# A gated mix of an S4 convolution and a GEGLU network: the feed-forward's gate and up products moved beside the making of K, and folded input spectra

## The chip, the cores and the metric

The kernel runs on one core of a Trainium2 chip. The metric is the device time of one execution in microseconds (us). A span is the same execution as the profile sees it; it is some 2 us shorter. Each run is labelled fast or slow. Only fast runs enter the ratios.

The engines are called as in the profile: PE multiplies matrices (PEld loads its weights), DVE works on vectors, ACT evaluates functions and copies, POOL here issues the indirect transfers, SP issues most DMA transfers (SPq is its queue).

## The reference

```python
x = A_u                                            # 1 x 2048 x 640, bf16
g = sigmoid((x * gate_w).sum(-1, keepdims=True))
K = einsum("dn,dnl,dn->dl", C, exp(dt*A*l), dt*B).real      # 640 channels, 128 complex modes each
y = irfft(rfft(x padded to 4096) * rfft(K padded to 4096))[:2048]   # per channel
a = y + x * Dskip
b = (gelu(x @ w_gate) * (x @ w_up)) @ w_down       # 640 -> 1728 -> 640
return g * a + (1 - g) * b
```

Both kernels make K from tables of exponentials and sines (ACT), scale them (DVE), and contract over the 128 modes with very small matmuls (PE), 160 channels at a time. The convolution is done with four blocks of 512 tokens: spectra of x (called U) and of K by matmuls with a table of cosines and sines, products of spectra on DVE, and an inverse transform by matmuls again.

## The kernel before

K is made first, with the transform of x beside it. The contraction of 160 channels is 320 matmuls, each of 21 columns with a weight load of its own. Its result is copied and laid out anew by 16 small transfers.

```python
    def contract(ch):                                   # called four times
        ...
        for hb in range(2):
            for g in range(gh):
                for q in range(2):
                    for j in range(4):
                        d = G4 * j + gh * hb + g
                        nc.tensor.matmul(psK[32 * j:32 * j + 32, hb, NX2 * g:NX2 * g + NX2], lhsT=cs1[:, q, :, d],
                                         rhs=cs2[:, q, :, d], start=(q == 0), stop=(q == 1))

    def k_out(ch):
        ...                                             # two ACT copies out of PSUM
        for j in range(4):
            for q in range(4):
                na = 6 if q == 0 else 5
                eng = nc.gpsimd if ch == NCH - 1 and j >= 2 else nc.sync
                eng.dma_start(out=Kt[32 * q:32 * q + 32, 0:na, CH * ch + G4 * j:CH * ch + G4 * j + G4],
                                  in_=kst[32 * j:32 * j + 32, q:NX2:4, :])
```

The transform of x takes 256 matmuls with four row blocks each (`for k in range(4)`). When K is there, DVE forms the products of the spectra while PE does gate and up for one block of 512 tokens after the other:

```python
    for tq in range(NB):
        ...
        for ft in range(NFT):
            ...
            gate(tq, ft, Gs[:])                         # five matmuls, then gelu on ACT
            pU = psU.tile([128, 512], FP32, name="pU")
            for kt in range(NKT):
                nc.tensor.matmul(pU[:], lhsT=Wu[:, kt, f0:f0 + 128], rhs=xT[tq][:, kt, :],
                                 start=(kt == 0), stop=(kt == NKT - 1))
            nc.scalar.copy(out=Us[:], in_=pU[:])
            nc.vector.tensor_tensor(out=ht[:, ft, :], in0=Gs[:], in1=Us[:], op=ALU.mult)
```

Last come `down` (28 matmuls per tile of 128 tokens) and the inverse. The inverse uses a symmetry: 128 matmuls give a tile and its mirror image, DVE adds and subtracts the halves, and the mirrored rows are stored by indirect transfers from POOL.

## Time and profile before

The time before is 405.9 us in the median (403.6 to 406.6, four runs). The page of the profiled run begins as follows. The first lines give busy time, share and instructions of each engine. The rows below cut the span into 40 slices, and each digit is a busy share in tenths; PEclk is the granted clock of PE.

```profile
span 404.8 us, 7313 instructions
PE 311.0 (77%) x2903; PEld 181.4 (45%) x2918; DVE 322.1 (80%) x628; ACT 232.8 (58%) x369; POOL 29.0 (7%) x49
...
PE   0556557453565775689999999999999699999993
...
DVE  8979816998765995945999999999994567777753
ACT  7999989858999647347666557465457200100000
...
PEclk9959886665967678679999999999999999999998
```

The windows view gives the same by stage. Its columns are named in its first line.

```profile
core 0: us, PE busy (x) PEld busy (x) DVE busy (x) ACT busy (x) POOL busy (x), PEclk, DMA share, GB/s
...
80.00:120.00 40.00, 22.54 (x579) 16.03 (x572) 33.84 (x79) 33.58 (x66) 0.00 (x0) 0.68 0.17 44
120.00:156.00 36.00, 24.75 (x403) 15.29 (x402) 26.43 (x58) 26.16 (x31) 0.29 (x1) 0.72 0.34 100
...
205.00:313.00 108.00, 103.86 (x541) 49.42 (x551) 103.17 (x151) 64.37 (x108) 3.64 (x4) 1.00 0.07 17
313.00:324.00 11.00, 6.90 (x44) 4.20 (x43) 5.63 (x11) 3.48 (x7) 2.29 (x2) 1.00 0.81 255
324.00:388.00 64.00, 63.99 (x472) 46.10 (x472) 46.20 (x88) 3.84 (x9) 10.36 (x10) 1.00 0.16 52
```

| stage of before, us | what bounds it |
|---|---|
| 0 to 177, K | ACT (busy 142 us) and DVE (138). PE is busy 99 us, at a mean clock of 0.75 |
| 177 to 313, products beside gate and up | both PE (104 of the last 108 us) and DVE (103) |
| 313 to 324 | the load of w_down (DMA share 0.81) |
| 324 to 398, down and inverse | PE, busy 73.8 of 74 us |

### The profile page before, as it was taken

How to read it: one execution, taken by the hardware profiler on the slowest of the kernel's cores; microseconds unless marked ns; L12 is line 12 of the kernel's file. 1: busy time of each engine (PE TensorE's matmuls, PEld its weight loads, DVE VectorE, ACT ScalarE, POOL GpSimd, SP SyncE). 2: the span in 40 equal slices, each digit the busy share in tenths (PEclk: the TensorE clock that was granted, in tenths of full speed). 3: DMA queues.
4: the chain of work that ended last, by engine and by line, in shares of the span. 5: the costliest groups of instructions: out<-in, count | busy, mean ns of one | idle time of the engine just before them, and what ended most of it. 6: DMA issues, size and time to landing. Idle time of an engine off the chain costs nothing.

```text
span 404.8 us, 7313 instructions
## 1 busy us (share of the span) xinstructions
PE 311.0 (77%) x2903; PEld 181.4 (45%) x2918; DVE 322.1 (80%) x628; ACT 232.8 (58%) x369; POOL 29.0 (7%) x49
## 2 busy tenths in 40 slices
PE   0556557453565775689999999999999699999993
PEld 0324222343433454435545445444444377777771
DVE  8979816998765995945999999999994567777753
ACT  7999989858999647347666557465457200100000
POOL 4000000000000001400000000000002204120000
PEclk9959886665967678679999999999999999999998
DMA  6422200021113035372001100100011802121000
GB/s 113 147 78 66 66 6 0 2 70 21 56 27 85 6 105 170 68 215 52 22 0 34 33 1 2 32 2 0 8 34 33 275 27 90 64 68 49 34 34 33
DMA packets 37507, 22.57 MB, mean 56 GB/s; under 512 B 28832, under 2 KB 33632, under 8 KB 37472
## 3 DMA queue, kind: packets, MB, share of 16 engines
q1 hardware_dynamic: 36448, 19.36, 17.6%
q0 software_dynamic: 1024, 2.73, 2.1%
q8 instruction: 23, 0.38, 0.4%
q14 instruction: 12, 0.10, 0.1%
HBM read 14.99 MB, written 2.62 MB: 44 GB/s over the span
## 4 chain that ended last, share of the span: by engine, by line
DVE 33%; PE 32%; ACT 19%; DMA 6%; SPq 5%; issue 4%; POOLq 0%; POOL 0%; ACTq 0%
PE pD L767 13%; PE pG L515 6%; DVE arena L479 5%; DVE arena L478 5%; ACT arena L378 4%; ACT arena L333 4%; PE pU L711 4%; ACT arena L261 3%; DVE arena L715 3%; DVE arena L476 3%; DVE arena L475 3%; PE pY L776 3%; DMA arena<-in_B_w_down_dram 3%; PE psK L410 2%; SPq L424 2%
## 5 line engine op out<-in xcount | busy, mean ns | idle before, releaser
L227 PE MATMUL pT<-arena 128*128 128x320 bf16 x256 | 53.3, 372 | 42.6 <-ACT arena L261 30.0
L515 PE MATMUL pG<-arena 128*128 128x512 bf16 x257 | 65.6, 389 | 4.2 <-DMA arena<-arena 2.2
L711 PE MATMUL pU<-arena 128*128 128x512 bf16 x250 | 65.1, 384 | 1.9 <-DMA arena<-in_B_w_up_dram 1.3
L767 PE MATMUL pD<-arena 128*128 128x320 bf16 x448 | 62.8, 299 | 1.9 <-DMA arena<-in_B_w_down_dram 1.9
L227 PEld LDWEIGHTS <-arena 128*128 128x128 bf16 x256 | 30.2, 119 | 64.6 <-issue 34.9
L767 PEld LDWEIGHTS <-arena 128*128 128x128 bf16 x448 | 43.8, 98 | 19.1 <-issue 2.1
L378 ACT ACTIVATE arena<-arena 128x2240 bf16<-128x2240 int16 (+1 forms) x20 | 43.6, 2180 | 12.0 <-DVE arena L370 7.1
L780 ACT COPY arena<-pY 128x320 f32<-128x320 f32 x16 | 6.8, 426 | 75.7 <-PE pY L776 75.7
L517 ACT ACTIVATE arena<-pG 128x512 bf16<-128x512 f32 x52 | 31.2, 600 | 27.4 <-PE pG L515 26.9
L713 ACT CAST arena<-pU 128x512 bf16<-128x512 f32 x52 | 30.4, 587 | 23.2 <-PE pU L711 21.7
L515 PEld LDWEIGHTS <-arena 128*128 128x128 bf16 x260 | 26.0, 100 | 35.5 <-issue 7.7
L711 PEld LDWEIGHTS <-arena 128*128 128x128 bf16 x260 | 25.3, 98 | 30.5 <-DMA arena<-in_B_w_up_dram 2.2
L410 PE MATMUL psK<-arena 128*32 128x21 bf16 x1280 | 20.7, 213 | 22.9 <-DVE arena L395 8.8
L478 DVE TENSOR_TENSOR arena<-arena 128x1280 bf16<-128x1280 bf16 (+5 forms) x40 | 32.5, 814 | 0.5 <-ACT arena L444 0.5
L479 DVE TENSOR_TENSOR arena<-arena 128x1280 bf16<-128x1280 bf16 (+5 forms) x40 | 32.6, 816 | 0.3
L410 PEld LDWEIGHTS <-arena 128*32 128x32 bf16 x1280 | 20.0, 153 | 24.6 <-issue 15.6
L367 DVE SCALAR_TENSOR_TENSOR arena<-arena 128x160 int32<-128x160 f32 x84 | 20.8, 319 | 11.3 <-ACT arena L378 11.3
L438 PE MATMUL pT<-arena 128*128 128x320 bf16 x144 | 26.7, 318 | 3.3 <-ACT arena L444 2.2
L769 DVE SCALAR_TENSOR_TENSOR arena<-pD,omg,arena 128x320 f32<-128x320 f32 x32 | 17.5, 547 | 14.5 <-PE pD L767 14.5
L444 ACT CAST arena<-pT 128x640 bf16<-128x640 f32 (+1 forms) x40 | 22.6, 592 | 8.0 <-PE pT L438 4.5
L715 DVE TENSOR_TENSOR arena<-arena 128x512 bf16<-128x512 bf16 x52 | 21.5, 414 | 7.0 <-ACT arena L713 7.0
L261 ACT ACTIVATE arena<-pT 128x640 bf16<-128x640 f32 x32 | 21.9, 699 | 5.0 <-PE pT L227 4.3
(97 smaller groups left out, 418.3 us busy)
## 6 DMA issues: line engine op xcount, KB each, us to landing
arena<-in_A_u_dram SPq DMA_DIRECT2D x16, 320.0 KB, 3.3
arena<-in_B_w_gate_dram SPq DMA_DIRECT2D x1, 2160.0 KB, 9.5
arena<-in_B_w_down_dram SPq DMA_DIRECT2D x1, 2080.0 KB, 10.5
arena<-in_B_w_up_dram SPq DMA_DIRECT2D x1, 1360.0 KB, 6.3
arena<-in_A_u_dram SPq DMA_DIRECT2D x8, 160.0 KB, 2.3
out_dram<-arena SPq DMA_DIRECT2D x8, 160.0 KB, 1.8
arena<-in_B_w_up_dram SPq DMA_DIRECT2D x1, 800.0 KB, 5.5
arena<-arena SPq DMA_DIRECT2D x42, 12.5 KB, 1.9
```

The costliest lines, as they stand in the source:

```text
L227: nc.tensor.matmul(pU[:, h, 0:DH], lhsT=tab[:, k, q, fsl(ft)], rhs=ublk[f0, b][:, k, h * DH:(h + 1) * DH], start=(k == 0), stop=(k == 3))
L261: nc.scalar.activation(out=Uf[ft][:, q, b, :].rearrange("p (h d) -> p h d", h=2), in_=pU[:, :, 0:DH], func=ACT.Copy, scale=1.0 / S)
L378: nc.scalar.activation(out=dst, in_=ph_tile(nph[ch, g])[:].bitcast(I16)[:, :, 0:n, 0:2 * CH:2], func=ACT.Sin, scale=SIN_SCALE)
L410: nc.tensor.matmul(psK[32 * j:32 * j + 32, hb, NX2 * g:NX2 * g + NX2], lhsT=cs1[:, q, :, d], rhs=cs2[:, q, :, d], start=(q == 0), stop=(q ...
L478: nc.vector.tensor_tensor(out=t1[:, 0:nb, :], in0=U[:, 1 - q, 0:nb, ds], in1=g[1], op=ALU.mult)
L479: nc.vector.tensor_tensor(out=dst, in0=dst, in1=t1[:, 0:nb, :], op=op1)
L515: nc.tensor.matmul(pG[:], lhsT=Wg[:, kt, 128 * ft:128 * ft + 128], rhs=xT[tq][:, kt, :], start=(kt == 0), stop=(kt == NKT - 1))
L517: nc.scalar.activation(out=out, in_=pG[:], func=ACT.Gelu_apprx_tanh)
L711: nc.tensor.matmul(pU[:], lhsT=Wu[:, kt, f0:f0 + 128], rhs=xT[tq][:, kt, :], start=(kt == 0), stop=(kt == NKT - 1))
L713: nc.scalar.copy(out=Us[:], in_=pU[:])
L715: nc.vector.tensor_tensor(out=ht[:, ft, :], in0=ht[:, ft, :] if early else Gs[:], in1=Us[:], op=ALU.mult)
L767: nc.tensor.matmul(pD[:, 0:DH], lhsT=HT[c][:, ft, 256 * r + par:256 * r + 256:2], rhs=Wd[:, ft, hs], start=(ft == 0), stop=(ft == NFT - 1))
```

## The change

The intent is to fill the half idle PE of the first stage with gate and up, and to pair the products of spectra with the PE work that comes last. All three main engines get a fixed order: a planner places each piece of work by a modelled duration, and a script fixes the sequence of ACT's function tables. The diff is over a thousand lines; this is its core, by hand, with cuts marked.

```diff
+    ctx.enter_context(tc.manual_schedule(engines={ENG.Activation, ENG.DVE, ENG.PE}))
+    plan = Plan()                       # pe(), ve(), ac(), dma(), pool() add pieces with a duration
...
+    def burst(b, banks):                # gate for two of 14 column tiles, all four token blocks, then up
+        for f in (2 * b, 2 * b + 1):
+            for tq in range(NB):
+                gate(f, tq, banks)
...
+        for f in (2 * b, 2 * b + 1):
+            for tq in range(NB):
+                up(f, tq)               # of 8 up results 6 are read from PSUM by DVE, 2 go by an ACT copy
...
+    burst(5, six)
...
+    burst(6, six)
+    for c in range(2, 4):
+        for g in range(3):
+            Z()                         # sine
+            XM2(c, g)                   # scaling
+        contract(c)
...
+    # table of K's transform (FK, 2304 KB) and of cosines (1024 KB): written to DRAM early, read back here
+    dma(430, lambda: nc.sync.dma_start(out=FK..., in_=dFK[:]), r=["dFK"], w=["FK"], after=...)
+    # folded input: natural rows plus and minus mirrored rows
+            pool(1000, lambda ...: nc.gpsimd.indirect_dma_start(out=mir[b][:, h, :], ..., in_=u2[:, :], in_offset=...))
+        ve(..., tensor_tensor(out=pls[b][:], in0=nat[b][:], in1=mir[b][:], op=ALU.add))
+        ve(..., tensor_tensor(out=nat[b][:], in0=nat[b][:], in1=mir[b][:], op=ALU.subtract))
-                for k in range(4):      # transform of x: 256 matmuls
+                        for j in range(2):   # 128 matmuls
...
+    for c in (3, 2, 1, 0):              # products of spectra, block by block, in place of U
+        for ft in range(NF):
+            product(c, ft, hs)
...
-                pE ... e in range(2)    # inverse by symmetric halves, 128 matmuls, mirrored indirect stores
+    for i in range(16): down(i, order[i])
+    for i in range(16): inverse(i, order[i])   # 256 matmuls, 96 small ones for Dskip, plain stores
+    script = [("trig", 8), ("exp", 6), ("gelu", 5), ("sqrt", 1), ("gelu", 3), ("trig", 2), ...]
+    plan.run(script, prio)
+    plan.emit()
```

## The prediction

> **What bounds the kernel now.** The windows view splits the 404.8 us span in three. To about 205 us K is made: ACT is busy 160 us and DVE 160 us, PE only 127 us at a granted clock of 0.59 to 0.83 until 176 us. From 205 to 313 us the chain of waits is nearly all DVE products, DVE busy 50 of 50 us, with PE's gate and up products beside them. From 313 us PE bounds: a 10.5 us wait for w_down, then 28 matmuls of 3.80 us and 8 of 1.09 us alternating to 388 us. After the last indirect store is issued (391.6 us) 13 us pass.
>
> **The change.** Gate and up (about 1.08 us per group of 5 matmuls, 108 groups or 117 us) move into the K stage, whose PE is half idle. The products then run beside w_down and the inverse transform, not beside gate/up.
>
> Stage A, K plus gate/up, at start-to-start rates from the chain (2,560-column sin 2.3, 320-column exp 0.36, 512-column eviction 0.5, bf16 2,560-column multiply 1.40 us):
> - ACT: sins 41, tables 8, exps 38, FK copies 9, gelus 29, a quarter of the up copies 7, rest 7, and about 25 table loads (10 now) of 1.28 us, 32: sum 171 us.
> - DVE: phases 44, scaling 48, setup 26, up multiplies 33 (three quarters read PSUM directly; a 64-row one of that form took 689 ns, against 414 from SBUF): about 153 us.[...]
> - PE: 117 + contraction 23 + FK 9 + logits 3 = 152 us[...].[...] I expect 0.85 to 0.95 in this stage.
> With ACT about 90% occupied, A ends near 197 us. The last sin, multiply, contraction and K relayout (12 us in the present chain, 156 to 168) end near 211 us.
>
> Stage B: folding halves the U transform's matmuls (256 to 128, minus 17 us of PE) but adds 6 us of DVE and waits for 8 mirrored indirect loads (1.08 us each). Spectra need 64 copies of 0.63 us on ACT, 40 us, of which some 33 come after K is complete: 245 us. The w_down load, which reuses FK's place, lands about 11 us later. Then PE has 16 x 3.80 = 61 us of down and 41 us of inverse (256 matmuls instead of 128, since the symmetric halves are no longer combined, plus the Dskip diagonals): to about 357 us. DVE products keep their volume (about 113 us, as now) and end near 340 us, so they hide behind PE. Plain stores should shorten the end from 13 to about 6 us.
>
> **Predicted 362 us, 8 in 10 within 342 to 385.** Faster by over 2%: 0.95; within 2%: 0.04; slower: 0.01.
>
> **What would show it.** After: PE clock above 0.85 in the first 190 us; ACT the busiest engine there, with about 25 table loads; the last gelu near 195 us; DVE nearly solid between 215 and 340 us; PE without gaps from about 257 us; products' busy time unchanged within 5%; U-transform matmuls halved; a chain that is ACT early, PE late.
>
> **What would make it wrong.** The fixed orders come from modelled durations: if DVE serves up's two PSUM banks late, PE stalls[...] and A stretches (towards 385). If bursts mesh better, A ends at 180 us (towards 342). If products, not PE, end last, the chain will show DVE to the end. If the mirrored loads or the K relayout land late, everything in B shifts by as much.

The sum goes from 197 (stage A) to 211 (K) and 245 us (spectra), then 11 us for w_down and 61 + 41 us of PE, to about 357, and with about 6 us at the end to 362, within the rounding. What before shows is a clock of 0.59 to 0.83 in windows of 15 to 21 us from 20 to 176 us, with PE busy 46 to 85% of each, of 1.00 in the first 20 us, with PE busy 27%, and of 1.00 from 205 to 313 us, with PE busy 104 of 108 us.

## More of the kernel before

One more excerpt matters: the end of the making of K, in the timeline view of before. Its columns are start, duration, engine, kernel line, operation, and in brackets the idle time before it and what ended that. L378 is the sine, L410 the contraction, L418 the copy out of PSUM, L424 the small transfers.

```profile
156.29 2.09 ACT L378 ACTIVATE arena<-arena 128x2240 bf16<-128x2240 int16 x1
156.44 11.92 SPq L424 DMA_DIRECT2D arena<-arena  x16
...
159.79 3.48 PE L410 MATMUL psK<-arena 128*32 128x21 bf16 x225 [4.45 <-DVE arena L395]
...
164.53 1.59 PE L410 MATMUL psK<-arena 128*32 128x21 bf16 x95 [1.26 <-issue]
166.17 0.92 ACT L418 CAST arena<-psK 128x420 bf16<-128x420 f32 x2 [6.60 <-PE psK L410]
...
169.09 5.48 SPq L424 DMA_DIRECT2D arena<-arena  x8
...
176.62 0.52 POOL L722 MEMSET arena<- 64x512 bf16 x1 [4.38 <-DMA arena<-arena]
```

The last sine ends at 156.29 + 2.09 = 158.4 us. The 16 transfers that start at 156.44 belong to the third contraction. The fourth takes 159.79 to 166.12, and of its 16 transfers SP issues 8 until 174.6; K is in place at 176.6. So 18.2 us pass between the last sine and K, and the third contraction's transfers fall beside the fourth contraction.

## The result, and the profile after

The time after is 382.9 us in the median (382.3 to 383.0, four runs), against 405.9 for before beside it. The ratio is 0.944 (95% interval 0.940 to 0.948). Ratios here and below are the mean time of one kernel's fast runs over that of the other's of the same rounds, so not quite the ratio of the quoted medians. The direction was right, and 382.9 lies inside the range of 342 to 385, but 21 us above the predicted 362.

The same lines of the page, of after:

```profile
span 380.8 us, 7329 instructions
PE 312.5 (82%) x3002; PEld 184.4 (48%) x3014; DVE 300.0 (79%) x527; ACT 228.8 (60%) x351; POOL 23.4 (6%) x38
...
PE   0158797789988899999975659994599999979996
...
DVE  8595768179997949979977048799999999999632
ACT  5999683899999898899971357996012121200000
...
PEclk9999899899996989999975687999599999999999
```

Note the hole in all three rows a little past the middle, with a dip of the clock to 0.5. It is where most of the missing 21 us went. The windows view of after shows the stages:

```profile
80.00:120.00 40.00, 37.03 (x534) 20.09 (x537) 39.03 (x93) 39.05 (x54) 0.00 (x0) 0.96 0.14 31
...
195.00:228.00 33.00, 19.19 (x505) 13.69 (x499) 14.62 (x23) 12.41 (x24) 11.95 (x15) 0.66 0.44 122
228.00:262.00 34.00, 33.38 (x222) 22.39 (x222) 29.88 (x42) 30.81 (x54) 0.63 (x1) 0.93 0.12 24
262.00:271.00 9.00, 0.15 (x1) 0.13 (x2) 8.86 (x7) 1.38 (x3) 0.00 (x0) 0.78 0.79 230
271.00:352.00 81.00, 78.63 (x577) 55.77 (x576) 79.49 (x87) 12.70 (x16) 0.00 (x0) 0.96 0.09 17
```

In this stretch of the first stage (80 to 120 us) PE, DVE and ACT are now all over 90% busy at once (37, 39 and 39 of 40 us), at a clock of 0.96 where it had been 0.68. From 271 us PE's down runs beside DVE's products (79 and 79 of 81 us). The 108 us of before in which gate and up stood beside products are gone. What was paid for that: K is there only at 228 us, where it was 177; the spectra after it (228 to 262) overlap little else; and PE's last stage takes 271 to 377 us, 106 us against 74 (324 to 398; 34 matmuls of the inverse, 4.8 us, came before that), mostly because the inverse has 256 matmuls in place of 128, some 17 us by their starts (8 in 1.08 us), and 96 small ones.

Between 195 and 228 us no engine is half busy but PE. The timeline of after shows why. L468 is the sine, L521 the contraction, L526 the copy out of PSUM, L534 the small transfers, L840 the spectrum of K. The lines are chosen from many; `x136` means 136 matmuls in a row.

```profile
191.16 4.04 ACT L468 ACTIVATE arena<-arena 128x2240 bf16<-128x2240 int16 x2
191.32 2.53 PE L521 MATMUL ps<-arena 128*32 128x21 bf16 x136
...
201.43 0.27 PE L521 MATMUL ps<-arena 128*32 128x21 bf16 x4 [0.44 <-issue]
...
205.10 3.76 PE L521 MATMUL ps<-arena 128*32 128x21 bf16 x243 [0.52 <-issue]
...
205.19 0.51 ACT L526 CAST arena<-ps 128x420 bf16<-128x420 f32 x1 [7.22 <-remote]
205.73 20.65 SPq L534 DMA_DIRECT2D arena<-arena  x24
...
213.04 1.01 PE L521 MATMUL ps<-arena 128*32 128x21 bf16 x56 [4.18 <-issue]
...
228.41 3.89 PE L840 MATMUL ps<-arena 128*128 128x320 bf16 x14 [4.66 <-DMA arena<-arena]
```

The last sine ends at 195.2, and K is in place at 228.4, which is 33.2 us later. Two contractions, which after take 6.5 us each where they stand alone (measured on the first, 112.72 to 119.19 us), here take from 191.3 to 214.1 us, 22.7 together. In the middle PE goes forward one to five matmuls every 0.74 us (called the trickle from here on); later it stands for 4.18 us waiting for "issue", that is, for nothing that the profile shows. By count, the last matmul of the third contraction starts near 200 us, but ACT's copy of its second half starts only at 205.19, and SP gets no word of it sooner. SP then issues 24 small transfers one after another, 20.65 us. The waits of SP's queue in this stretch hold one line that concerns them:

```profile
SPq L534 <- DMA arena<-dFK: 3.8, 1, 3.8
```

So SP stood 3.8 us until the reload of FK had landed, which it had issued just before.

### The profile page after: what moved, and what is told of

Its sections match the earlier page's. It is cut to its first block, busy times and chain, and to the rows that moved or that the text cites. A ratio compares the mean times of both kernels' runs of the same rounds, so it can differ in the third digit from the quotient of the medians.

```text
span 380.8 us, 7329 instructions
## 1 busy us (share of the span) xinstructions
PE 312.5 (82%) x3002; PEld 184.4 (48%) x3014; DVE 300.0 (79%) x527; ACT 228.8 (60%) x351; POOL 23.4 (6%) x38
## 4 chain that ended last, share of the span: by engine, by line
DVE 33%; PE 32%; ACT 14%; SPq 10%; issue 6%; DMA 3%; DVEq 0%; ACTq 0%
DVE arena L879 24%; PE ps L575 8%; SPq L294 6%; PE ps L521 6%; PE ps L964 6%; PE ps L596 5%; ACT arena L468 3%; PE ps L820 3%; ACT arena L427 2%; SPq L299 2%; DMA dFK<-arena 2%; DVE arena L857 2%; PE ps L840 2%; ACT arena L846 2%; DVE arena L454 2%
## 5 line engine op out<-in xcount | busy, mean ns | idle before, releaser
L879 DVE TENSOR_TENSOR arena<-arena 128x640 bf16<-128x640 bf16 (+4 forms) x112 | 110.1, 1012 | 2.3
L575 PE MATMUL ps<-arena 128*128 128x512 bf16 x275 | 72.6, 412 | 30.0 <-DMA arena<-in_A_u_dram 24.1
L943 PE MATMUL ps<-arena 128*128 128x320 bf16 x448 | 64.1, 307 | 9.4 <-DMA arena<-in_B_w_down_dram 9.4
L596 PE MATMUL ps<-arena 128*128 128x512 bf16 x254 | 61.3, 388 | 4.3 <-ACT arena L603 1.8
L947 ACT ACTIVATE arena<-ps,omg 128x640 bf16<-128x640 f32 x16 | 12.7, 793 | 60.1 <-PE ps L943 60.1
L468 ACT ACTIVATE arena<-arena 128x2240 bf16<-128x2240 int16 (+1 forms) x20 | 43.1, 2175 | 0.9 <-DVE arena L457 0.8
L964 PE MATMUL ps<-arena 128*128 128x320 bf16 x256 | 37.4, 299 | 2.1 <-DVE arena L973 1.9
L607 DVE TENSOR_TENSOR arena<-ps,arena 128x512 bf16<-128x512 f32 x38 | 25.6, 685 | 14.6 <-PE ps L596 14.5
L521 PE MATMUL ps<-arena 128*32 128x21 bf16 x1280 | 23.0, 214 | 12.6 <-issue 12.3
L579 ACT ACTIVATE arena<-ps 128x512 bf16<-128x512 f32 (+1 forms) x56 | 29.1, 614 | 3.6 <-PE ps L575 3.4
L521 PEld LDWEIGHTS <-arena 128*32 128x32 bf16 x1280 | 20.8, 152 | 15.8 <-issue 15.8
L840 PE MATMUL ps<-arena 128*128 128x320 bf16 x144 | 22.6, 318 | 4.7 <-DMA arena<-arena 4.7
L846 ACT CAST arena<-ps 128x640 bf16<-128x640 f32 (+1 forms) x40 | 21.0, 621 | 6.4 <-PE ps L840 6.1
L973 DVE SCALAR_TENSOR_TENSOR arena<-ps,g_f,arena 128x640 bf16<-128x640 f32 x16 | 14.1, 880 | 13.0 <-PE ps L968 13.0
L824 ACT ACTIVATE arena<-ps 128x640 bf16<-128x640 f32 x32 | 19.9, 799 | 2.2 <-PE ps L820 2.2
```

The lines of the kernel that those rows point to most:

```text
L468: ac(actns(2 * n * w), lambda: nc.scalar.activation(out=dst, in_=ph.bitcast(I16)[:, :, :, 0:2 * w:2], func=ACT.Sin, scale=SIN_SCALE), r=[( ...
L521: nc.tensor.matmul(ps[32 * j:32 * j + 32, 6 + hb, NX2 * g:NX2 * g + NX2], lhsT=cs1[ch % 2][:, q, :, d - c0], rhs=cs2[ch % 2][:, q, :, d - ...
L575: nc.tensor.matmul(ps[:, k, :], lhsT=Wg[f % 2][:, kt, :], rhs=xT[tq][:, kt, :], start=(kt == 0), stop=(kt == NKT - 1))
L579: ac(actns(512), lambda: nc.scalar.activation(out=HT[f][0:p, tq, :], in_=ps[0:p, k, :], func=ACT.Gelu_apprx_tanh), r=[("bank", k)], w=[("H ...
L596: nc.tensor.matmul(ps[:, 4 + k, :], lhsT=Wu[f % 2][:, kt, :], rhs=xT[tq][:, kt, :], start=(kt == 0), stop=(kt == NKT - 1))
L607: ve(tt(512, 1) + 60, lambda: nc.vector.tensor_tensor(out=HT[f][:, tq, :], in0=ps[:, 4 + k, :], in1=HT[f][:, tq, :], op=ALU.mult), r=[("ba ...
```

## The experiments

The theory at the start: K comes late because the two contractions run out of instructions and are slowed by the transfers beside them (mirrored loads, the reload of FK). It was a conjecture from after's profile, which puts 12.3 of the 12.6 us that PE idles before matmuls of the contractions down to "issue". The rivals: ACT bounds the first stage through its 26 table loads, so that everything shifts with it; SP's queue of small transfers is what bounds; or the end is set by PE's inverse and K's arrival matters little. A text that numbers its theories says what they are; where it doesn't, the first is the theory given here.

Each experiment is an edit of the kernel after. It was timed against before on the same chip, so variants are compared through before's ratio; after itself stood at 0.944. The jobs ran on several chips: e1 to e4 on chip 5, e5 to e8 on 14, e9 to e11 on 12, e12 on 11; after's chip isn't on record, and after was not run again beside its variants. This matters for what is called the trickle below. Edits marked "wrong" change the result.

### e1_mirror_plain: no indirect loads (wrong)

```diff
-            pool(1000, lambda b=b, h=h, k=k: nc.gpsimd.indirect_dma_start(out=mir[b][:, h, :], ...))
+            pool(1000, lambda b=b, h=h, k=k: nc.sync.dma_start(out=mir[b][:, h, :], in_=u2[S*b+256+h:S*b+512:2, :]))
```

> Changed kernel with the 8 mirrored (indirect, POOL-queue) loads of U replaced by plain strided loads of the same rows on the SP queue; instruction order of PE, DVE and ACT unchanged; the result is wrong on purpose. In the changed kernel the last two contractions take 22.7 us (191.3 to 214.1 us) instead of about 6.5 us each; from 197.5 to 205 us PE gets 3 to 5 matmuls per 0.74 us, and that ends when the last indirect load has been issued. Theory 1 (PE is short of instructions because the indirect loads compete with its instruction fetch): the trickle vanishes, the contractions end near 206 us, K is complete near 220 us, total about 7 us less (376). Theory 2 (the trickle has another cause, or the relayout queue alone sets K's completion): the trickle stays or K is complete at 227 us as before, total within 1.5 us of 383.

Measured: 376.1 us (373.4 to 377.9), ratio 0.926 (0.921 to 0.931). The trickle is gone. In its place stand bursts of exactly 128 with gaps, as the timeline of this run shows:

```profile
196.45 2.08 PE L521 MATMUL ps<-arena 128*32 128x21 bf16 x128 [2.42 <-issue]
...
200.18 2.07 PE L521 MATMUL ps<-arena 128*32 128x21 bf16 x128 [1.65 <-issue]
...
206.65 2.07 PE L521 MATMUL ps<-arena 128*32 128x21 bf16 x128 [4.40 <-issue]
```

K is in place at 223.1, 5.3 us earlier. Without the indirect loads the contraction still stalls. That the loads as such cost the 5.3 us isn't shown: e11 below keeps them, lacks the trickle all the same, and has K at 221.9.

### e2_no_fk_reload: the FK table isn't read back (wrong)

```diff
-    dma(430, lambda: nc.sync.dma_start(out=FK..., in_=dFK[:]), r=["dFK"], w=["FK"], ...)
+    dma(430, lambda: None, r=["dFK"], w=["FK"], ...)
```

> Changed kernel without the 2,304 KB reload of the FK table (stale data is read there, so the result is wrong on purpose); nothing else changes. Theory 1 (late transfers starve PE of instructions): the 4.2 us issue gap in the last contraction (208.9 to 213.0 us) goes, but the trickle before it stays. Theory 2 (the relayout of K waits in the SP queue behind the reload): the relayout's transfers of the third chunk, of which 9 were issued and 7 held until 215 us, run through. Either way K is complete about 4 to 8 us earlier, total 375 to 379. If neither is so and K is late only because stage A is, total stays at 383.

Measured: 375.8 us (375.0 to 376.5), ratio 0.928 (0.924 to 0.932). The trickle stays, the gap of 4.18 us before the last 56 matmuls falls to 0.83, and SP's 24 small transfers take 16.26 us instead of 20.65. K is in place at 221.4, 7.0 us earlier, and the time falls by 7.1.

### e3_both: both edits (wrong)

> Both edits at once (result wrong on purpose). Theory 1 plus 2: contractions take about 13 us together and end near 204 us, K is complete near 214 us, 13 us earlier; total 368 to 371. If the end of stage B is bound by PE work independent of K's completion, total falls by less than 5 us.

Measured: 373.0 us (370.3 to 374.8), ratio 0.919 (0.913 to 0.926). That is 10 us less than after. The two contractions took 189.3 to 207.7 us, so 18.4 us and not the 13 that twice 6.5 would give. Gaps of 3.09, 1.65, 1.65 and 1.66 us remain between bursts of 128:

```profile
195.47 2.08 PE L521 MATMUL ps<-arena 128*32 128x21 bf16 x128 [3.09 <-issue]
...
199.19 2.07 PE L521 MATMUL ps<-arena 128*32 128x21 bf16 x128 [1.65 <-issue]
...
202.92 2.07 PE L521 MATMUL ps<-arena 128*32 128x21 bf16 x128 [1.65 <-issue]
...
206.65 1.02 PE L521 MATMUL ps<-arena 128*32 128x21 bf16 x56 [1.66 <-issue]
```

e1, which differs from this run by the reload alone, has a gap of 4.40 us where the longest after the first is 1.66 here. K is in place at 217.5, 10.9 us earlier than in after; 2.1 of these were there already when the third contraction began (at 189.3 instead of 191.3). Whether the rest of the stall needs a competitor is what e6 tests.

### e4_gelu_copy: gelu replaced by a copy (wrong)

```diff
-func=ACT.Gelu_apprx_tanh
+func=ACT.Copy
```

> Changed kernel with gelu replaced by a plain copy in the evictions of gate (result wrong on purpose): ACT's order is otherwise the same, but 16 of the 26 table loads of 1.28 us vanish. If ACT bounds stage A (my prediction's reading): stage A and everything after it end 16 to 20 us earlier, total 363 to 367. If PE, DVE or the DMA queue bound it as much: less than 8 us gained, total over 375.

Measured: 377.1 us (374.7 to 379.1), ratio 0.932 (0.926 to 0.939). 16 of the 26 table loads are gone and ACT's busy time falls from 228.8 to 207.5 us, by 21.3 us, but the time falls by about 6. The last sine ends at 188.2, 7 us earlier; the contractions then take 24 us (184.3 to 208.3). So ACT does not bound the first stage alone, and the late K goes with the contractions wherever they stand.

### e5_exp_early and e7_exp_split: orders meant to part the two contractions (both correct)

```diff
 script (both):
-    ("trig", 2), ("gelu", 9), ("trig", 1), ("gelu", 7), ("trig", 3), ("exp", 4), ("gelu", 6), ("trig", 2), ("gelu", 2)
+    ("trig", 2), ("gelu", 9), ("exp", 4), ("trig", 1), ("gelu", 7), ("trig", 3), ("gelu", 6), ("trig", 2), ("gelu", 2)
 e7 alone: the early write of FK to DRAM in three parts, each as soon as its part is made
```

> Correct version of the changed kernel in which only the order of ACT's activation sets is edited: the last four exp steps (sigmoid and the three blocks of the second exp grid) run before the two last groups of sins, not after them. The third contraction can then run beside gate and up work, some 15 us earlier, instead of directly before the fourth, and the FK reload moves with it, off the last contraction and off the relayout queue. If K's lateness comes from the two contractions standing back to back among stage B's transfers (theory 1, instruction supply): K complete near 215 us instead of 227, total 369 to 374. If stage A merely shifts the work (rival): total within 2 us of 383.

> The order edit of the run before, and the spill of the FK table to DRAM in three parts, each sent when its own eighteen-part share is made, instead of one 2,304 KB transfer after all of it (correct result). In the changed kernel ACT stood 5.0 us and PE 3.8 us waiting for this spill near 60 to 69 us. If that wait is on the path: 3 to 5 us less than the order edit alone. If later slack takes it up: under 1.5 us less.

Measured: e5 377.3 us (375.5 to 380.1), ratio 0.931 (0.925 to 0.937); e7 374.2 us (372.7 to 376.6), ratio 0.927 (0.921 to 0.933). e5 missed its aim: the contractions stayed back to back, since the last gate burst owns the PSUM banks that they need. e7's median is some 3 us lower than e5's, but the two intervals overlap, so the worth of the split write isn't shown. e7 is correct, and has the lowest ratio of the correct versions (e12, at 0.928, is level with it): its interval does not meet after's (0.940 to 0.948). One run of before in this job took 779 us; it was slow and left out.

### e6_contract_twice: the first contraction issued twice (correct)

```diff
-                for g in range(GH):
+                for g in [*range(GH)] * (2 if ch == 0 else 1):
```

> Changed kernel with the first chunk's contraction issued twice in a row (640 small matmuls; same result), at about 112 us, where the DMA engines are nearly idle (share 0.12). It measures the supply of instructions by itself. If it is bounded by itself, not only by competing transfers: after the first 220 or so matmuls PE runs in bursts of 128 with gaps of about 1.65 us, as in the run with both late transfers taken away, so 640 take about 17 us. If only competing transfers starve it: one gap of 1.4 us per 320 as now, 640 take 13 us.

Measured: 390.6 us (two runs, 390.1 and 391.1), ratio 0.965 (0.959 to 0.972). The first contraction of after stands in a quiet place, so this makes 640 matmuls in a row without competitors. The timeline of this run:

```profile
111.83 3.40 PE L521 MATMUL ps<-arena 128*32 128x21 bf16 x220
116.24 2.06 PE L521 MATMUL ps<-arena 128*32 128x21 bf16 x128 [1.00 <-issue]
119.69 2.06 PE L521 MATMUL ps<-arena 128*32 128x21 bf16 x128 [1.39 <-issue]
123.42 2.05 PE L521 MATMUL ps<-arena 128*32 128x21 bf16 x128 [1.67 <-issue]
126.88 0.71 PE L521 MATMUL ps<-arena 128*32 128x21 bf16 x36 [1.41 <-issue]
```

After some 220 matmuls PE gets 128 every 3.45 to 3.73 us, though they take it 2.06. In the DMA view of the same stretch (111 to 128 us) a weight load of 160 KB moves from 111.9 to 113.0, beside the first row of matmuls; during the gaps nothing else does. The row has 40 slices of 0.43 us, and the lone ones are the transfers of queue 8, "instruction", five of them:

```profile
DMA  0049101000000010000000010000000100000001
...
q8 instruction: 5, 0.08, 2.0%
```

The whole page counts 26 packets on queue 8 for this kernel and 23 for after. The edit adds 320 matmuls and 320 weight loads, 640 instructions, which at 256 to a packet (the 128 matmuls of a burst and their 128 weight loads) are 2.5 packets. The trace holds the time of each packet (0.9 to 1.3 us in the table); next to it stands the time at which PE's small matmuls go on:

```
kernel   packet on queue 8, us      matmuls go on at    after landing
e6       113.80 to 114.80           116.24              1.44
e6       117.33 to 118.34           119.69              1.35
e6       120.81 to 122.09           123.42              1.33
e6       124.56 to 125.47           126.88              1.41
before   162.09 to 163.33           164.53              1.20
after    210.60 to 211.48           213.04              1.56
e7       199.65 to 200.59           201.96              1.37
e9       206.78 to 207.74           209.12              1.38
e9       216.34 to 217.44           218.88              1.44
```

Every gap listed ends 1.2 to 1.6 us after one packet has landed. The table is a choice; counted over all fourteen traces, PE pauses 83 times for more than 0.7 us between two small matmuls of a contraction with no other matmul between, and 80 of the pauses, short or long, end 1.2 to 1.7 us after a packet on queue 8 has landed. (Of the other three, before's at 97.86 waits for DVE, e8's at 114.55 for ACT by the profile, and e2's at 204.80 is the end of the trickle.) So what the profile calls "issue" in these lines goes with the landing of a packet on queue 8; "supply of instructions" means no more than that below.

### e8_gelu_last: the overlap undone (correct)

```diff
-    script = [("trig", 8), ("exp", 6), ("gelu", 5), ("sqrt", 1), ("gelu", 3), ("trig", 2), ("gelu", 8), ...]
+    script = [("trig", 8), ("exp", 6), ("sqrt", 1), ("trig", 5), ("exp", 3), ("trig", 6), ..., ("gelu", 56), ("exp", 1)]
 cut: the gate bursts keep to four PSUM banks, and the sigmoid moves to the end
```

> Undoes the overlap alone: ACT's script is edited so that all gelus come after the last sin (gate can then use four PSUM banks only and waits; the sigmoid moves to the end); the rest of the changed kernel stays, correct result. K is then made alone by about 150 us and gate/up follow alone at PE's pace, about 117 to 125 us, with only up's multiplies on DVE. If the move of gate/up beside K is what pays: total 415 to 440. If it is not (gain from folded spectra and shorter end): total under 395.

Measured: 469.5 us (two runs, 467.6 and 471.3), ratio 1.160 (1.151 to 1.170), so 87 us slower than after and beyond the 415 to 440 expected. The last contraction ends at 177 us, not by about 150; gate and up take 177 to 293, the rest lasts to 465. The windows view of this run shows PE standing idle while DVE and ACT work:

```profile
60.00:100.00 40.00, 0.00 (x0) 0.13 (x1) 39.38 (x90) 37.23 (x61) 0.00 (x0) 0.50 0.00 0
```

The overlap is what pays: the rest of the change without it is slower than before by 16%. (This run is not before itself, which had gate and up beside the products of spectra.) In this window, without a single matmul, PE's granted clock is 0.50; in after's window of 80 to 120 us, with PE busy 37 of 40 us, it is 0.96.

### e9_apart_a and e10_apart_b: the third and fourth contraction parted (both correct)

```diff
 e9  (on e7):  script ..., ("trig", 2), ("gelu", 9), ("exp", 4), ("trig", 3), ("gelu", 13), ("trig", 3), ("gelu", 2)
-    burst(6, six)
+    burst(6, four)
 e10 (on e7):  script ..., ("trig", 2), ("gelu", 7), ("exp", 4), ("trig", 3), ("gelu", 9), ("trig", 2), ("gelu", 6), ...
               burst(6, four), and DVE's scaling first in priority
```

> Correct version: the split spill, the order of activation sets edited so that the third chunk's sins come in one group before 13 gelus and the fourth's after them, and the last gate burst kept to four PSUM banks so that the third contraction needn't wait for it. On PE the third and fourth contractions now stand 60 large matmuls apart; before this edit they stood back to back (640 small matmuls) in every variant. Theory 1 (instruction supply: 128 small matmuls per some 3.7 us once the stock of about 220 is used, slower still beside stage B's transfers): both contractions take 7 to 9 us, K is complete 10 us or more earlier than in the changed kernel's 227.6, total 362 to 368. Rival (K's time set by stage A's other work, order of contractions irrelevant): total as with the split spill and order edit before, 374.

> As the run before, but with the activation sets in six groups instead of four and the scaling multiplies given the highest priority on DVE, so that the third contraction comes earlier still, 80 large matmuls before the fourth, and some up products follow the fourth. Theory 1: total 360 to 368; whichever of the two is faster shows how much the exact place matters. Rival: 374.

Measured: e9 386.7 us (385.5 to 387.8), ratio 0.955; e10 416.6 us (415.6 to 417.6), ratio 1.027. Both missed. In e9 the third contraction ran clean (179.58 to 185.68, 6.1 us), and its 16 small transfers were done by 201.6, as hoped. But the first stage ended later, and the fourth contraction (203.0 to 219.9) then fell beside the mirrored loads:

```profile
209.12 2.09 PE L521 MATMUL ps<-arena 128*32 128x21 bf16 x128 [3.91 <-issue]
...
218.88 1.02 PE L521 MATMUL ps<-arena 128*32 128x21 bf16 x56 [7.67 <-issue]
```

By the table above, the packet that ended the gap of 7.67 us itself took 1.1 us, but it started 7.2 us after the burst before the gap had begun (209.12 to 216.34); in the quiet e6 that was 1.1 us (116.24 to 117.33). So the delay lies before the packet's start. In that stretch (209 to 217 us) the DMA view counts 63 and 52% of the 16 engines' time for the packets of the two data queues (115% together, so the times of some packets overlap). In e10 DVE waits 28.9 us for sines in its scaling lines and the first stage stretches: the last sine ends at 224.5 us, 29 us later than in after.

### e11_half_inverse: half the matmuls of the inverse (wrong)

```diff
-                    for q in range(2):      # in inverse()
+                    for q in range(1):
```

> Changed kernel with half of the inverse transform's matmuls (only one of the two parts, 128 instead of 256 as in the kernel before; the result is wrong on purpose); order otherwise unchanged. It measures what giving up the combined symmetric halves costs. If PE bounds the end, as predicted: the ten inverses that stand after the last product shrink from 2.45 to 1.37 us, total 10 to 13 us less (370 to 373), no more, since the products' end near 352 us then bounds. If DVE bounds the end: within 3 us of 383.

Measured: 368.2 us (364.6 to 369.3), ratio 0.906 (0.900 to 0.912), 14.7 us less than after. Not all of it is the edit: in this profile K was in place at 221.9, 6.5 us earlier than in the profile of after, though the edit comes later in the order; the trickle was absent, on another chip than that of e1 to e4. From K to the end it took 144.5 us against 152.4, so the edit is worth about 8 us. It took 128 matmuls off PE, which by their starts in the timeline (8 in 1.08 us) are 17 us. PE then waits for DVE's mixes, the longest time here:

```profile
334.23 2.29 PE L964 MATMUL ps<-arena 128*128 128x320 bf16 x8 [6.61 <-DVE arena L973]
```

So at the end DVE is not far behind PE, and halving the inverse alone would win half of what it takes off PE.

### e12_queues: FK's reload and four small transfers moved to ACT's queue (correct, on e7)

```diff
-    nc.sync.dma_start(out=FK..., in_=dFK[:])
+    nc.scalar.dma_start(out=FK..., in_=dFK[:])
-                e = nc.sync if j < 2 or ch < NCH - 1 else nc.gpsimd
+                e = nc.scalar if j == 1 and ch == NCH - 1 else nc.sync if j < 2 or ch < NCH - 1 else nc.gpsimd
```

> Correct version: order edit and split spill as in the seventh run, whose instruction order on PE and DVE it keeps; in addition the FK reload and a quarter of the last chunk's relayout of K are issued from ACT's queue instead of SP's. In the seventh run SP issued the 24 relayout transfers of the last two chunks between 194.3 and 217.9 us, about 8 us more than 24 times 0.645 us, in part behind the reload, and K was complete at 219.6 us. Theory 2 (the relayout waits in the SP queue): K complete at 215 to 217 us, total 370 to 373 against 374. If the transfers themselves, or PE's supply of instructions, set the time: K complete at 219 us and total 374, or worse if ACT's copies are held up by issuing.

Measured: 377.6 us over six runs, two of them slow; the four fast ones average 375.9, ratio 0.928 (0.924 to 0.932), against e7's 0.927. No gain. Its profile is of a run labelled slow, so only the order of events is read from it: ACT's copy out of PSUM waited 8.2 us for the FK reload that it had issued itself, and the gaps before the bursts of the contraction stayed (4.25 and 3.03 us).

```profile
206.06 0.51 ACT L526 CAST arena<-ps 128x420 bf16<-128x420 f32 x1 [8.21 <-DMA arena<-dFK]
```

So e12 is no clean test of SP's queue: the wait for the reload moved to ACT. What the traces show of this rival is that the last link differs. In after SP's queue stands for nothing but the reload (3.8 us) from 205.73 to its last transfer, so there it sets K once it has begun; in e3 it stands 6.5 us for ACT's copy, so there the contraction does.

## Why the prediction was right or wrong

**K's arrival fixes the time.** The table sets the moment at which PE begins the spectrum that needs K's last columns against the span of the same run. (e8, e11 and e12 are left out: e8 has gate and up in between, e11 a shorter end, e12 a profile of a slow run.)

| kernel | PE begins on K's last columns, us | span, us | from K to the end |
|---|---|---|---|
| predicted | 211 | 362 (time) | 151 |
| after | 228.4 | 380.8 | 152.4 |
| e1 | 223.1 | 376.1 | 153.0 |
| e2 | 221.4 | 373.3 | 151.9 |
| e3 | 217.5 | 371.7 | 154.2 |
| e4 | 220.8 | 372.7 | 151.9 |
| e5 | 225.9 | 378.1 | 152.2 |
| e6 | 236.0 | 388.1 | 152.1 |
| e7 | 219.6 | 370.6 | 151.0 |
| e9 | 229.3 | 383.6 | 154.3 |
| e10 | 260.4 | 415.1 | 154.7 |

In the rows after to e7 PE stood idle 1.3 us or more just before, waiting for K; there K's arrival differs by 18.5 us (217.5 to 236.0), and the rest takes 151 to 154 us. In e9 and e10 PE did not wait for K at this point (0.31 us idle). In e10 SP had issued K's last small transfer by 243.9 us, and PE came to the spectra of K at 257.3, after the late transform of x; so e10's 260.4 isn't K's arrival, though the rest is as long from there. So the rival by which the inverse sets the end whatever K does has fallen: the inverse adds to K's arrival. The prediction had the second part right, 151, and the first wrong, 211 instead of 228.4. These 17.4 us, the 1.4 of the second part and the 2.1 by which the time exceeds the span make up the 20.9 us.

**The step that failed** was: "The last sin, multiply, contraction and K relayout (12 us in the present chain, 156 to 168) end near 211 us." It failed twice.

- *A misreading.* In before's own trace 18.2 us pass from the last sine to K, not 12. The 11.92 us that I took from the chain are the third contraction's transfers, which before issues beside the last sine and the fourth contraction.
- *What the new order does to it.* In after the third and fourth contraction stand back to back at the very end, so SP has 24 transfers to issue after the third is done, and PE has 640 small matmuls in a row. The third's result was taken at 205.2 instead of some 198 (191.3 plus 6.5). SP then needed 20.65 us, of which it waited 3.8 for the FK reload. Add 2 us for the last landing: 228.4.

In the prediction's own terms, the last sine was put at 211 less 12, or 199, and ended at 195.2 (3.8 us early); the chain from there to K was put at 12 and took 33.2 (21.2 too long). The difference of the two is the 17.4 us. Of the 21.2, 6.2 are the misreading (18.2 less 12). The other 15.0 can be split by the same stretch in other runs. It takes 28.3 us in e1, so 4.9 go with the trickle, which e1 lacks; 24.3 in e3, so 4.0 more go with the FK reload. (Taken the other way round, by e2's 26.4, it is 6.8 for the reload and 2.1 for the trickle.) Of the 6.1 that remain, 5.4 go with the supply of instructions (gaps of 3.09, 1.65, 1.65 and 1.66 us in e3): the contractions of e3 took 18.4 us and not 13, and SP waited 6.5 us for the copy that follows them. e6, with no data moving during its gaps, took 15.8 us for the same 640 matmuls, so 2.8 of the 5.4 need no other transfer; e3 still had plain loads of x beside its first gap. The remaining 0.7 us is not resolved. The prediction had named the kind of risk ("If the mirrored loads or the K relayout land late, everything in B shifts by as much"), without a size.

**How far the cause is shown.** That the gaps before bursts of 128 end with a packet on queue 8 is read from 80 of 83 gaps in fourteen traces. That a packet of 16 KiB holds 256 instructions is the author's estimate, from bursts of 128 matmuls with 128 weight loads between one packet and the next, and from 26 packets in e6 where after has 23 and 640 instructions fewer, and 22 in e11, which has 256 fewer than after. That data transfers lengthen the gaps is shown by e1 against e3 (4.40 against 1.66 us, the reload alone taken away) and by the gap that e2 shortens from 4.18 to 0.83 us; that it is the packet's start that they delay is read from one gap alone, e9's 7.2 us against e6's 1.1. The trickle of one to five matmuls per 0.74 us is *not* explained by it: in after packets landed at 197.9 and 202.2 us, in the middle of the trickle, and it went on to 205. It is present in after, e2 and e4, there while the indirect loads are being issued (in after gaps from 194.1 to 205.1 us, loads from 190.0 to 204.1), and absent in e1 and e3, which have no indirect loads. But it is also absent in e5, e6, e7, e9, e11 and e12, whose contractions have the indirect loads beside them as well; e11 has even the order of after up to there. All these ran on other chips (14, 12 and 11) than e1 to e4 (chip 5). So in the profiles from chip 5 the trickle comes with the loads, in those from the other three chips it doesn't, and the chip, or whatever else differs between the jobs, is a rival that no run tests. The cause of the trickle stays open. So does the question why ACT and SP in after see the third contraction done 5 us after its last matmul ("remote" in the profile); both end together at 205.1.

**The other steps.**

- "ACT about 90% occupied, A ends near 197": the last sine ended at 195.2 and the last gelu at 198.0. Right. About 25 table loads: 26, of 1283 ns each, as in before (in after one runs from 29.47 to 30.75 us, between a square root that ends at 29.45 and a gelu that starts at 30.76). A PE clock of 0.85 to 0.95: 0.91 to 1.0 in the windows up to 195 us. Right. The prediction did lean on ACT as the bound; e4 shows that 21.3 us less of ACT give only 6. DVE and PE are about as full (37 and 39 of 40 us above), which fits, but was not tested.
- "689 ns for a product read from PSUM": 685 ns in the mean of 38 (128 by 512), against 421 from SBUF. Right.
- "Spectra, some 33 us after K": 228.4 to 261.8, 33.4. The wait for w_down, 11: 9.1. Right.
- "PE 61 + 41 us": 270.85 to 377.1, 106.3. 4 us too low. The starts of the 16 inverses lie 2.45 us apart, 39 us; down took 64 us, and there are small waits for DVE.
- "Products keep their volume": 121.9 us against 127.5 (sums of the groups in the groups view), within 5%. DVE was solid with them from 246 and not from 215, as they wait for K, and it ended 1 us after PE.
- "Plain stores should shorten the end from 13 to about 6": a second misreading. In before PE worked to 397.8, and the last store was issued at 400.4, so 4.4 us passed to the end at 404.8. After: 2.7 us from DVE's last mix to the end. The gain was under 2 us. This error (6 us put, 3.7 from PE's end to the end of the span) and the 1.9 us too much for w_down nearly cancelled the 4 us of PE, so that 151 came out as well as it did is partly luck.

**Where the expected gain went.** It was not lost to contention in the first stage, which meshed as hoped. It was given back at the seam: the plan put the 640 small matmuls, the 24 transfers that depend on them and the reloads for the next stage at the same moment, where little else can run: of PE's work that follows, only the transform of x (214.0 to 221.1 us) doesn't need K. e7 measures some 7 us less than after (ratio 0.927 against 0.944, of 405 us) without changing any arithmetic. Not all of that need be its order: K is there 8.8 us earlier in its profile, 4.2 because the third contraction begins earlier (187.15 instead of 191.32), and 4.6 because the stretch from there to K is shorter (32.4 us instead of 37.1), and e11, with after's order and no trickle, has 32.3 there as well. A run of after on e7's chip would tell; there is none.

## What to carry to other kernels

Before moving work to overlap, find the one event that the rest waits for, and read the chain to that event instruction by instruction in the timeline rather than from the summed chain; here a 12 us piece belonged to another contraction. Don't place long rows of very small matmuls beside big transfers at the seam of two stages: in these runs, outside the trickle, the first gap came after 136 (e6, at 201.04 us) to 261 of them (e9, at 179.58), and from there PE got 128 with their weight loads per 3.45 us at best (e6, at 116.24). And run the reference point again on each chip on which a variant runs; without that, what the trickle did to e5, e7 and e11 can't be told from their edits. A fixed order that fills three engines is worth much (87 us here), but look at what it bunches up at its end.
